# Weights loaded later, an opening in another order and an ending shared by two engines, in a recurrent-scan and gated-GLU kernel

## The chip, the cores and the metric

The kernel runs on one core of one Trainium2 chip. The metric is the device time of one execution in microseconds (us). A core has five engines that run side by side and wait for each other by semaphores: PE (matrix products), ACT (activations, copies with a scale), DVE (vector work), POOL (GpSimd, vector work out of on-chip memory) and SP (here it only issues DMAs). Each engine works through its own list of instructions strictly in order. PE's results land in eight PSUM banks, which ACT and DVE empty; POOL cannot read them.

## The reference

For x of 2048 tokens by 448 features (bfloat16), the kernel computes a diagonal complex recurrence and a gated two-layer network on the same normalised input, and joins them:

```
xn = layernorm(x)
Bu = xn @ B_bar.T                     # complex, 448 states; B_bar = (Lam_bar - 1) / Lam * B
h[t] = Lam_bar * h[t-1] + Bu[t]       # Lam_bar = exp(exp(log_dt) * Lambda)
s = 2 * Re(h @ C.T) + xn * Dskip
g = sigmoid(xn @ w_gate) * (xn @ w_up)        # 1792 wide
out = x + s * silu(g @ w_down)
```

## The kernel before, in words

**Tiling.** The 2048 tokens are four chunks `c` of 512 tokens; a chunk has four tiles `j` of 128 tokens. The 448 states are four blocks `pt` (three of 128, the last of 64 whose real and imaginary parts share the partitions). The 1792 hidden features are 14 blocks `ft` of 128.

**The recurrence without complex numbers.** Each state is turned by its own angle per token, so that the recurrence becomes a real one that DVE's scan does (`scan`, L597). The turning needs tables of cosines (`cosT`) and sines with both signs (`spm`) of 512 columns. They are built once: `emit_whole` or `frac_by` and `emit_frac` bring the angle into one turn, `emit_abs` takes its magnitude, `emit_sin` and `emit_cos` (ACT) give columns 256 to 511, `emit_neg` (L454, DVE) the negated sine, and `emit_mirror` (L457 to L460, POOL) copies the other half backwards.

**The products.** A pair of units runs on PE at a time (`duo`). A unit is either `gu_unit` (gate and up of one `ft`, 7 products each for upper and lower row halves) or `bu_unit` (Bu of one block `pt`). The upper 64 rows of one unit run beside the lower 64 of the other. Where a sum changes from one half to the other, the next product has to follow the other half's last one; the kernel brings this about with an instruction that does nothing on POOL (L520), which waits for PE and for which PE waits:

```
if self.half not in (None, half):
    word = pool.nop()
```

These words stand in POOL's list behind all that was written before them.

**Order of a chunk.** Chunk 0 opens with three, then four blocks by `gu_wholes` and `gu_halves` (L710, L703), then `emit_line(0, ...)`. Each later chunk runs gate/up units, Bu units, then `emit_downs` of the chunk before (the product with `w_down`, tile `wd`, sums `ds`) and `emit_ys` (the product with C, tile `ct`). DVE's work of the recurrence is cut into `pieces` that `fill` places between the units; `due` and `due_g` hold elementwise work that is written a little later. At the very end `keep_order` fixes the written order on every engine.

**Opening.** Tiles 0 and 1 of x are normalised with DVE's statistics (`ln_stats`), tiles 2 and 3 with ACT's sums (`ln_sum`, `ln_mean`, `ln_square`); POOL raises the variance to -1/2 (`ln_pow`, L238; `ln_pow_of` also adds the epsilon there, L246). `ln_norm` writes the normalised tile, `ln_turn` transposes it on PE into PSUM (`tps`, two banks) and `ln_out` (L280) copies it out. `rows` holds log_dt, Lambda_im and Lambda_re; PE transposes it into `tp_v`, and `emit_vecs` (L313) copies that. `warm` (L192) are products with the identity whose result nobody reads.

**Transfers.** Nearly all DMAs stand in SP's list, in written order. Among them, in the order before: x of chunk 0, weights in three parts (`load_w`), B, x of chunk 1, transposes of B (`emit_b`), the down weights (L1020), x of chunk 2, the transposes of chunk 1 (L270), C (`load_c`, planned at (0, 7)), the swap of the last block's halves (L538, L539), and the transposes of C (L169), which ACT (L490) scales and joins during the downs of chunk 0.

**End.** For the last chunk `empty` (L772) puts Silu on ACT; `emit_rest_of` (L847, L853) computes xn * Dskip * gate + x for tiles 0 to 2 on DVE; for each tile `emit_y` multiplies with C on PE and `emit_fin` (L865, L868, L869) multiplies the sum by the gate, adds the rest and sends the tile out. Tile 3 goes in two halves of 224 columns (3a, 3b below) and adds its skip part by a product with the identity on PE.

Of the kernel before, what the change touches and what calls it, by code (L numbers as in the profile page):

```python
# [10 lines left out]
FP32 = mybir.dt.float32  # L11
# [6 lines left out]
D = 448  # L18
F = 1792
P = 128  # L20
# [43 lines left out]
def kernel(  # L64
# [55 lines left out]
    def load_w(eng, f0, f1):  # L120
        for t, mat, p0 in ((wg, B_w_gate, 0), (wu, B_w_up, 64)):
            eng.dma_start(out=t[:, :, f0:f1], in_=mat[0:384, f0:f1].rearrange("(kt p) f -> p kt f", p=P))
            eng.dma_start(out=wt[p0:p0 + 64, f0:f1], in_=mat[384:448, f0:f1])

# [290 lines left out]
    def emit_whole(pt):  # L415
        whole = sp.tile([P, HC], I32, name="whole", tag=("ta", "tb")[pt % 2])
        act.activation(whole[:], iota_f[:], ACT.Copy, scale=K["turn"][:, pt:pt + 1])
        K[pt] = whole


    def frac_by(eng, pt, tag):
        t = sp.tile([P, HC], FP32, name="turns", tag=tag)
        eng.tensor_scalar(out=t[:], in0=iota_f[:], scalar1=K["turn"][:, pt:pt + 1], scalar2=None, op0=ALU.mult)
        f = sp.tile([P, HC], FP32, name="fracs", tag=tag)
        eng.tensor_scalar(out=f[:], in0=t[:], scalar1=MAGIC, scalar2=-MAGIC, op0=ALU.add, op1=ALU.add)
        eng.tensor_tensor(out=f[:], in0=t[:], in1=f[:], op=ALU.subtract)
        K[pt] = f

# [24 lines left out]
    def emit_neg(pt):  # L453
        dve.tensor_single_scalar(out=spm[:, pt, 1, HC:TC], in_=spm[:, pt, 0, HC:TC], scalar=-1.0, op=ALU.mult)  # L454

# [249 lines left out]

    def gu_wholes(c, ft, gt, ut, first, n0=0, n1=TC):
        f0, f1 = ft * P, (ft + 1) * P
        for t, wm in ((gt, wg), (ut, wu)):
# [53 lines left out]
    def emit_downs(c):  # L762
# [42 lines left out]

    def y_ops(c, j, rows, d0=0, d1=D, skipped=False):
        sl = slice(j * P, (j + 1) * P)
        o = [(ident[rows, :], xn[c % 3][rows, j, d0:d1], d0, d1)] if skipped else []
        for pt in range(3):
# [30 lines left out]

    rests = {}

    def emit_rest_of(c, j):
        if j == 3:
            return
        t = op_.tile([P, D], BF16, name="t_g", tag="zb", bufs=4)
        dve.tensor_tensor(out=t[:], in0=xn[c % 3][:, j, 0:D], in1=gs[c][:, j, :], op=ALU.mult)  # L847
        if not rests:
            for k, nm in ((0, "raw_re"), (2, "raw_im")):
                both = w.tile([P, 2, D], FP32, name="t_x", tag=nm)  # L850
                rests.update({k: both[:, 0, :], k + 1: both[:, 1, :]})
            del rests[3]
        dve.tensor_tensor(out=rests[j], in0=t[:], in1=x_t[c][:, j, :], op=ALU.add)  # L853

    def emit_y(c, j, d0=0, d1=D):
        ops = y_ops(c, j, slice(0, P), d0, d1, j not in rests)
        ys[c, j] = bank("y_ps", D)
# [4 lines left out]
    def emit_fin(c, j, d0=0, d1=D):  # L862
        tt = c * TPC + j
        sg = op_.tile([P, D], BF16, name="sg", tag="sigd", bufs=4)
        dve.tensor_tensor(out=sg[:, d0:d1], in0=ys[c, j][:, d0:d1], in1=gs[c][:, j, d0:d1], op=ALU.mult)  # L865
        o = op_.tile([P, D], BF16, name="o_l", tag="zb", bufs=4)
        also = rests[j] if j in rests else x_t[c][:, j, :]
        dve.tensor_tensor(out=o[:, d0:d1], in0=sg[:, d0:d1], in1=also[:, d0:d1], op=ALU.add)  # L868
        sync.dma_start(out=out_flat[tt * P:(tt + 1) * P, d0:d1], in_=o[:, d0:d1])  # L869
# [110 lines left out]
    for ft in range(4):  # L980
        gu_wholes(0, ft, *gus[ft], False, HC, TC)
    emit_frac(1)
    emit_abs(1)
    emit_steps()
    for pt in (0, 1, 3):
        emit_sin(pt)
        emit_cos(pt)
        emit_neg(pt)
        if pt == 0:
            emit_b_twice()  # L990
            emit_frac(3)
            emit_abs(3)
    emit_abs(2)
    ubs = [fp.tile([P, TC], BF16, name="ub") for _ in range(4)]
# [4 lines left out]
    for ft in range(4):  # L999
        gu_out(ft, gus[ft][0], ubs[ft])  # L1000
        up_copy(ft)
        if ft == 1:
# [128 lines left out]
```

## Time and profile before

| | us |
|---|---|
| median of 3 runs | 187.44 (187.14 to 188.24) |
| the profiled execution, whole | 186.7 |
| its span, first to last instruction | 184.6 |
| PE busy | 178.0 (96%) |
| DVE busy | 164.4 (89%) |
| ACT busy | 114.6 (62%) |
| POOL busy | 29.1 (16%) |

The span is what the timelines below count in, from 0; the 2.1 us between it and the profiled execution lie around it. The granted TensorE clock is 1.00 all through. The page says that PE's matmuls are pipelined and their ends modelled, so that a busy PE is not one at its peak; pauses are read from where a product starts. In a timeline a row gives the start, the time from first to last of the instructions merged in it, the engine, the line, the operation, output and inputs, shapes, their number, and in brackets how long the engine had been idle just before and what ended that. "PEld" is the load of a matmul's stationary operand; "POOLq" and "SPq" are what POOL's and SP's sequencers do themselves, such as the words of L520 and the issue of a DMA.

### The profile page before, as it was taken

The numbers are of one execution on the slowest core, as the hardware profiler recorded it, in microseconds if no ns is written. First come the engines' busy times: TensorE is split into PE (matmuls) and PEld (weight loads), VectorE is DVE, ScalarE is ACT, GpSimd is POOL, SyncE is SP. The second block draws the span as 40 slices with busy tenths as digits, with TensorE's granted clock in tenths as the row PEclk, the third lists the DMA queues.
The fourth block names the chain that finished last, engine by engine and source line by source line (L and its number), as shares of the span: only waits on it lengthen the run. The fifth ranks groups of instructions, "written<-read, shape, count | busy, mean of one in ns | idle before, by whom it ended". The sixth has DMA issues, their size and how long they took to land.

```text
span 184.6 us, 4475 instructions
## 1 busy us (share of the span) xinstructions
PE 178.0 (96%) x1706; PEld 101.4 (55%) x1706; DVE 164.4 (89%) x331; ACT 114.6 (62%) x238; POOL 29.1 (16%) x64
## 2 busy tenths in 40 slices
PE   6899999999999999999999999999999999999990
PEld 5676788545544444645554445545654445655560
DVE  3789979989999969999999999599999999699494
ACT  4889857899579686997367766067048657051300
POOL 3689368514000000004000000000000000000000
PEclk9999999999999999999999999999999999999999
DMA  5999999934332122011241010020000010020102
GB/s 152 301 317 219 253 351 190 236 78 99 82 78 57 28 45 87 4 51 51 48 71 28 4 28 0 4 99 0 5 14 14 4 24 10 0 80 23 28 25 75
DMA packets 27659, 15.07 MB, mean 82 GB/s; under 512 B 16243, under 2 KB 27638, under 8 KB 27638
## 3 DMA queue, kind: packets, MB, share of 16 engines
q1 hardware_dynamic: 27488, 14.67, 34.2%
q8 instruction: 13, 0.21, 0.5%
q10 hardware_dynamic: 150, 0.12, 0.2%
q14 instruction: 8, 0.07, 0.1%
HBM read 8.49 MB, written 1.84 MB: 56 GB/s over the span
## 4 chain that ended last, share of the span: by engine, by line
PE 83%; DVE 10%; DMA 3%; issue 1%; ACTq 1%; SPq 0%
PE g_ps L518 23%; PE u_ps L518 20%; PE d_ps L518 17%; PE bu L518 10%; PE y_ps L518 8%; DMA rows<-in_A_Lambda_re_dram 2%; PE g_ps L710 2%; PE u_ps L710 1%; DMA wsw<-wv 1%; DVE sg L865 1%; DVE o_t L835 1%; DVE t_x L853 1%; DVE o_l L868 1%; DVE hF L745 1%; DVE wv L658 1%
## 5 line engine op out<-in xcount | busy, mean ns | idle before, releaser
L518 PE MATMUL u_ps<-xnT,wu 64*128 64x512 bf16 x312 | 66.5, 376 | 0.0
L518 PE MATMUL g_ps<-xnT,wg 64*128 64x512 bf16 x312 | 59.4, 376 | 0.0
L748 ACT ACTIVATE sig<-g_ps 128x512 bf16<-128x512 f32 x52 | 29.3, 599 | 27.6 <-PE g_ps L518 27.6
L518 PE MATMUL bu<-xnT,bT 64*128 64x512 bf16 x196 | 45.3, 376 | 0.0
L518 PE MATMUL d_ps<-wd,hF 64*128 64x448 bf16 x448 | 43.9, 349 | 0.0
L518 PEld LDWEIGHTS <-hF 64*128 64x128 bf16 x448 | 24.9, 94 | 18.0 <-POOLq L520 0.7
L518 PEld LDWEIGHTS <-wu 64*128 64x128 bf16 x312 | 24.8, 94 | 17.1 <-POOLq L520 1.6
L518 PEld LDWEIGHTS <-wg 64*128 64x128 bf16 x312 | 22.0, 94 | 18.0 <-POOLq L520 2.7
L748 ACT CAST ub<-u_ps 128x512 bf16<-128x512 f32 x52 | 29.3, 609 | 0.0
L597 DVE TENSOR_TENSOR_SCAN wv<-r_col,st,ta 128x512 bf16<-128x512 f32 x18 | 22.6, 1275 | 0.1
L518 PE MATMUL y_ps<-ct,h 64*128 64x448 bf16 (+2 forms) x203 | 22.7, 343 | 0.0
L518 PEld LDWEIGHTS <-bT 64*128 64x128 bf16 x196 | 17.8, 94 | 7.7
L745 DVE TENSOR_TENSOR hF<-sig,ub 128x512 bf16<-128x512 bf16 x52 | 20.9, 416 | 1.2 <-ACT ub L748 1.0
L518 PE MATMUL g_ps<-xnT,wt 64*128 64x512 bf16 x52 | 19.6, 376 | 0.0
L518 PE MATMUL u_ps<-xnT,wt 64*128 64x512 bf16 x52 | 19.6, 376 | 0.0
L518 PEld LDWEIGHTS <-h 64*128 64x128 bf16 (+1 forms) x203 | 13.3, 95 | 8.2 <-issue 0.4
L578 ACT CAST bus<-bu 128x512 bf16<-128x512 f32 x24 | 14.5, 603 | 2.9 <-PE bu L518 2.9
L776 ACT ACTIVATE sigd<-d_ps 128x448 bf16<-128x448 f32 x12 | 6.6, 552 | 14.1 <-PE d_ps L518 14.1
L238 POOL TENSOR_TENSOR rsd<-ve,mhalf 128x4 f32<-128x4 f32 (+2 forms) x6 | 6.5, 1080 | 47.5 <-PE u_ps L518 40.4
L518 PEld LDWEIGHTS <-wt 64*128 64x128 bf16 x104 | 9.8, 94 | 5.0
L835 DVE TENSOR_TENSOR o_t<-y_ps,xn 128x448 bf16<-128x448 f32 x12 | 6.9, 618 | 3.5 <-PE y_ps L518 3.4
L591 DVE TENSOR_TENSOR ta<-ta,tb 128x1024 bf16<-128x1024 bf16 x12 | 8.3, 690 | 0.3
(162 smaller groups left out, 223.5 us busy)
## 6 DMA issues: line engine op xcount, KB each, us to landing
wd<-in_B_w_down_dram SPq DMA_DIRECT2D x1, 1568.0 KB
x<-in_A_x_dram SPq DMA_DIRECT2D x3, 448.0 KB, 6.9
out_dram<-o_t SPq DMA_DIRECT2D x6, 224.0 KB, 2.1
wg<-in_B_w_gate_dram SPq DMA_DIRECT2D x2, 384.0 KB, 4.5
wu<-in_B_w_up_dram SPq DMA_DIRECT2D x2, 384.0 KB, 4.9
wg<-in_B_w_gate_dram SPq DMA_DIRECT2D x1, 576.0 KB
wu<-in_B_w_up_dram SPq DMA_DIRECT2D x1, 576.0 KB, 7.0
bsw<-bus SPq DMA_DIRECT2D x8, 64.0 KB, 2.0
```

Of the source, the lines that this page charges most:

```text
L238: pool.tensor_tensor(out=rsd[:, t:t + n, :], in0=ve[:, t:t + n, :], in1=mhalf[:, 0:n, :], op=ALU.pow)
L518: m = pe.matmul(self.t[:, n0:n1], lhsT=lhsT, rhs=rhs, start=self.done == 1, stop=self.done == self.n)
L578: empty = [lambda cc=cc: act.copy(out=bus[:, cc, :], in_=pst[cc][:]) for cc in range(2)]
L591: dve.tensor_tensor(out=T["ta"][:], in0=T["ta"][:], in1=T["tb"][:], op=add)
L597: dve.tensor_tensor_scan(out=T["wv"][:, cc, :], data0=rb, data1=T["ta"][:, cc, :], initial=(0.0 if c == 0 else st[pt][:, cc, :]), op0=mul, ...
L658: dve.tensor_tensor_scan(out=T["wv"][:], data0=rb, data1=T["ta"][:], initial=(0.0 if c == 0 else st3[:]), op0=mul, op1=add)
L710: pe.matmul(t[:, n0:n1], lhsT=wm[:, kt, f0:f1], rhs=xnT[c][:, kt, n0:n1], start=(first and kt == 0), stop=(not first and kt == 2))
L745: dve.tensor_tensor(out=h[:], in0=sig[:], in1=ub[:], op=ALU.mult)
L748: u.empty = [lambda: act.activation(sig[:], gt[:], ACT.Sigmoid), lambda: act.copy(out=ub[:], in_=ut[:])]
L776: act.activation(sigd[:], ds[j][:], ACT.Sigmoid)
L835: dve.tensor_tensor(out=o[:, i, :], in0=ys[c, j + 2 * i][:], in1=xb[:, i, :], op=ALU.add)
L853: dve.tensor_tensor(out=rests[j], in0=t[:], in1=x_t[c][:, j, :], op=ALU.add)
```

## The change

The diff, with lines of mere plumbing left out:

```diff
     def load_w(eng, f0, f1):
-        for t, mat, p0 in ((wg, B_w_gate, 0), (wu, B_w_up, 64)):
+        for t, mat in ((wg, B_w_gate), (wu, B_w_up)):
             eng.dma_start(out=t[:, :, f0:f1], in_=mat[0:384, f0:f1].rearrange("(kt p) f -> p kt f", p=P))
+        for mat, p0 in ((B_w_gate, 0), (B_w_up, 64)):
             eng.dma_start(out=wt[p0:p0 + 64, f0:f1], in_=mat[384:448, f0:f1])
...
-    act.dma_start(out=x_t[0][:, 1, :], in_=x_src[:, 1, :])
+    sync.dma_start(out=x_t[0][:, 1, :], in_=x_src[:, 1, :])
...
-    def load_c():
+    def load_wd_c():
+        sync.dma_start(out=wd[:], in_=B_w_down.rearrange("(ft p) d -> p ft d", p=P))
...
-        whole = sp.tile([P, HC], I32, name="whole", tag=("ta", "tb")[pt % 2])
+        whole = sp.tile([P, HC], I32, name="whole", tag=("ta", "tb", "tcs", "tb")[pt])
...
-    def frac_by(eng, pt, tag):
...
     def emit_neg(pt):
-        dve.tensor_single_scalar(out=spm[:, pt, 1, HC:TC], in_=spm[:, pt, 0, HC:TC], scalar=-1.0, op=ALU.mult)
+        pool.tensor_single_scalar(out=spm[:, pt, 1, HC:TC], in_=spm[:, pt, 0, HC:TC], scalar=-1.0, op=ALU.mult)
...
+                if c == NCH - 1:
+                    if q == 2:
+                        pieces.pop(0)[1]()
+                    emit_gate()
+                    emit_gate()
...
     def emit_rest_of(c, j):
-        if j == 3:
-            return
+        eng = dve if j % 2 == 0 else pool
         t = op_.tile([P, D], BF16, name="t_g", tag="zb", bufs=4)
-        dve.tensor_tensor(out=t[:], in0=xn[c % 3][:, j, 0:D], in1=gs[c][:, j, :], op=ALU.mult)
+        eng.tensor_tensor(out=t[:], in0=xn[c % 3][:, j, 0:D], in1=gs[c][:, j, :], op=ALU.mult)
...
-        dve.tensor_tensor(out=rests[j], in0=t[:], in1=x_t[c][:, j, :], op=ALU.add)
+        eng.tensor_tensor(out=rests[j], in0=t[:], in1=x_t[c][:, j, :], op=ALU.add)
...
     def emit_fin(c, j, d0=0, d1=D):
-        dve.tensor_tensor(out=o[:, d0:d1], in0=sg[:, d0:d1], in1=also[:, d0:d1], op=ALU.add)
+        (pool if j == 1 else dve).tensor_tensor(out=o[:, d0:d1], in0=sg[:, d0:d1], in1=rests[j][:, d0:d1], op=ALU.add)
...
-    warm(26)
-    for t in range(2):
-        ln_stats(t)
-        ln_pow_of(t, 1, mv[:, t:t + 1, 1:2], 1.0)
+    warm(31)
+    ln_stats(0)
+    ln_pow_of(0, 1, mv[:, 0:1, 1:2], 1.0)
+    ln_stats(1)
+    ln_root(1, 1)
     ln_sum(2)
-    ln_sum(3)
     turn_twice(tp_v, rows, 3)
-    warm(6)
...
-    ln_mean(2, 2)
+    ln_mean(2, 1)
     ln_square(2)
-    ln_square(3)
-    warm(4)
+    ln_pow_of(2, 1, sums[:, 2:3, 1:2], 1.0 / D)
     ln_norm(0, 1)
     ln_turn(0, 1)
     warm(4)
     ln_out(0)
     ln_out(1)
+    ln_stats(3)
+    for pt in (0, 1, 3, 2):
+        emit_whole(pt)
     act.activation(K["r"][:], K["arg"][:], ACT.Exp)
-    for pt in (1, 3):
-        emit_whole(pt)
     act.activation(dummy[:], hpi[:], ACT.Silu)
-    ln_pow_of(2, 2, sums[:, 2:4, 1:2], 1.0 / D)
-    frac_by(dve, 0, "ta")
-    emit_abs(0)
-    frac_by(pool, 2, "tcs")
+    ln_pow_of(3, 1, mv[:, 3:4, 1:2], 1.0)
     gus = [(bank("g_ps"), bank("u_ps")) for _ in range(3)]
     for ft in range(3):
-        gu_wholes(0, ft, *gus[ft], True, 0, HC)
-    for j in (2, 3):
-        ln_norm(0, j)
-        ln_turn(0, j)
+        gu_wholes(0, ft, *gus[ft], True, 0, HC, (0,))
+    for ft in range(3):
+        gu_wholes(0, ft, *gus[ft], True, 0, HC, (1,))
+    ln_norm(0, 2)
+    ln_turn(0, 2)
+    emit_frac(0)
+    ln_norm(0, 3)
+    ln_turn(0, 3)
+    emit_abs(0)
+    emit_frac(1)
+    emit_abs(1)
     for j in (2, 3):
         ln_out(j)
+    emit_frac(3)
+    emit_abs(3)
+    emit_frac(2)
+    emit_abs(2)
...
-    emit_frac(1)
-    emit_abs(1)
     emit_steps()
     for pt in (0, 1, 3):
         emit_sin(pt)
         emit_cos(pt)
-        emit_neg(pt)
         if pt == 0:
             emit_b_twice()
-            emit_frac(3)
-            emit_abs(3)
-    emit_abs(2)
...
-    emit_neg(2)
     for pt in (0, 1, 3, 2):
+        emit_neg(pt)
         emit_mirror(pt)
...
-        if pt == 2:
-            sync.dma_start(out=wd[:], in_=B_w_down.rearrange("(ft p) d -> p ft d", p=P))
...
-    at(0, 7, 0.0, load_c)
+    at(0, 7, 0.0, load_wd_c)
```

What it does:

- **Opening, transfers.** Tile 1 of x moves from ACT's list to SP's second place, so that the three `rows` are first on ACT's. In each part of the weights the two large transfers stand ahead of the two small ones.
- **Opening, normalisation.** The variance of tile 1 is prepared on DVE (`ln_root`), tile 2 alone is summed by ACT, tile 3 gets DVE's statistics and a power of its own on POOL. All gate products of the first three blocks stand ahead of their up products.
- **Opening, tables.** All four blocks take `emit_whole` on ACT and `emit_frac` on DVE; the three-step `frac_by` of blocks 0 (DVE) and 2 (POOL) is gone. The four negations go from DVE to POOL, each ahead of its block's mirrors.
- **Down weights.** Their transfer goes from between the transposes of B to behind the transposes of chunk 1, just ahead of C.
- **End.** In the downs of the last chunk, rests 0 and 2 are written on DVE right behind their Silu, ahead of the last two steps of the recurrence; rests 1 and 3, with the one of tile 3 new, on POOL. The last addition of tile 1 is POOL's. Tile 3 no longer uses the identity product.

More of the change, by code (lines that the diff above doesn't have):

```diff
@@ L415, in emit_whole @@
     def emit_whole(pt):
-        whole = sp.tile([P, HC], I32, name="whole", tag=("ta", "tb")[pt % 2])
+        whole = sp.tile([P, HC], I32, name="whole", tag=("ta", "tb", "tcs", "tb")[pt])
         act.activation(whole[:], iota_f[:], ACT.Copy, scale=K["turn"][:, pt:pt + 1])
         K[pt] = whole
-    def frac_by(eng, pt, tag):
[L422 to L427, printed above, removed]
     def emit_frac(pt):
@@ L704, in gu_halves, with gu_wholes @@
                       rhs=xnT[c][p0:p0 + 64, 3, n0:n1], start=first, stop=not first)
-    def gu_wholes(c, ft, gt, ut, first, n0=0, n1=TC):
+    def gu_wholes(c, ft, gt, ut, first, n0=0, n1=TC, which=(0, 1)):
         f0, f1 = ft * P, (ft + 1) * P
-        for t, wm in ((gt, wg), (ut, wu)):
+        for t, wm in [((gt, wg), (ut, wu))[i] for i in which]:
             for kt in range(3):
@@ L804, with y_ops @@
     ys = {}
-    def y_ops(c, j, rows, d0=0, d1=D, skipped=False):
+    def y_ops(c, j, rows, d0=0, d1=D):
         sl = slice(j * P, (j + 1) * P)
-        o = [(ident[rows, :], xn[c % 3][rows, j, d0:d1], d0, d1)] if skipped else []
+        o = []
         for pt in range(3):
@@ L838, in emit_two @@
         sync.dma_start(out=out_t[:, c * TPC + j:(c + 1) * TPC:2, :], in_=o[:])
-    rests = {}
+    rests, room_of_rests = {}, {}
     def emit_rest_of(c, j):
-        if j == 3:
-            return
+        eng = dve if j % 2 == 0 else pool
         t = op_.tile([P, D], BF16, name="t_g", tag="zb", bufs=4)
-        dve.tensor_tensor(out=t[:], in0=xn[c % 3][:, j, 0:D], in1=gs[c][:, j, :], op=ALU.mult)
+        eng.tensor_tensor(out=t[:], in0=xn[c % 3][:, j, 0:D], in1=gs[c][:, j, :], op=ALU.mult)
         if not rests:
@@ L850, in emit_rest_of @@
                 both = w.tile([P, 2, D], FP32, name="t_x", tag=nm)
-                rests.update({k: both[:, 0, :], k + 1: both[:, 1, :]})
-            del rests[3]
-        dve.tensor_tensor(out=rests[j], in0=t[:], in1=x_t[c][:, j, :], op=ALU.add)
+                room_of_rests.update({k: both[:, 0, :], k + 1: both[:, 1, :]})
+        rests[j] = room_of_rests[j]
+        eng.tensor_tensor(out=rests[j], in0=t[:], in1=x_t[c][:, j, :], op=ALU.add)
     def emit_y(c, j, d0=0, d1=D):
-        ops = y_ops(c, j, slice(0, P), d0, d1, j not in rests)
+        ops = y_ops(c, j, slice(0, P), d0, d1)
         ys[c, j] = bank("y_ps", D)
@@ L865, in emit_fin @@
         dve.tensor_tensor(out=sg[:, d0:d1], in0=ys[c, j][:, d0:d1], in1=gs[c][:, j, d0:d1], op=ALU.mult)
-        o = op_.tile([P, D], BF16, name="o_l", tag="zb", bufs=4)
-        also = rests[j] if j in rests else x_t[c][:, j, :]
-        dve.tensor_tensor(out=o[:, d0:d1], in0=sg[:, d0:d1], in1=also[:, d0:d1], op=ALU.add)
+        if j == 3:
+            o = sp.tile([P, D], BF16, name="o_l", tag="ctmp")
+        else:
+            o = op_.tile([P, D], BF16, name="o_l", tag="zb", bufs=4)
+        (pool if j == 1 else dve).tensor_tensor(out=o[:, d0:d1], in0=sg[:, d0:d1], in1=rests[j][:, d0:d1], op=ALU.add)
         sync.dma_start(out=out_flat[tt * P:(tt + 1) * P, d0:d1], in_=o[:, d0:d1])
```

## The prediction

> **What bounds the kernel now.** First the engines' shares and the chain that ended last (parts 1 and 4 of the page), then the waits by total time.
>
> ```profile
> PE 178.0 (96%) x1706; PEld 101.4 (55%) x1706; DVE 164.4 (89%) x331; ACT 114.6 (62%) x238; POOL 29.1 (16%) x64
> PE 83%; DVE 10%; DMA 3%; issue 1%; ACTq 1%; SPq 0%
> PEld L518 <- POOLq L520: 5.0, 15, 0.5
> ```
>
> PE bounds it: from 7.69 us (first product) to 180.46 its matmuls follow each other without a pause of over 0.4 us. So an opening shorter by some time is a kernel shorter by that, a PE pause anywhere is paid in full, and the end behind PE's last sums counts on its own. The third line is the one to keep in mind: L520 is the Pool `nop` that stands between the two row halves of a sum, so a matmul waits until Pool's queue has come to it. POOL is 16% busy over the span, but not where these words stand first. The timelines of the weight loads, DVE and POOL show it:
>
> ```profile
> 16.37 0.33 DVE L454 TENSOR_SCALAR spm<-spm 128x256 bf16<-128x256 bf16 x1
> 16.81 0.42 PEld L518 LDWEIGHTS <-wg 64*128 64x128 bf16 x6 [0.40 <-POOLq L520]
> 19.34 0.66 POOL L353 TENSOR_SCALAR smT<-sn 128x4 f32<-128x4 f32 x1
> 20.10 0.42 PEld L518 LDWEIGHTS <-wg 64*128 64x128 bf16 x6 [0.49 <-POOLq L520]
> ```
>
> The last table's negation ends on DVE at 16.70; the mirror L459 behind it in Pool's queue waits for that, the first `nop` stands behind the mirrors, and the weights load at 16.81. The next `nop` stands behind smT (ends 20.00), and PE goes on at 20.10. Twice PE lost some 0.2 us here to Pool's queue, although three mirrors were only queued, not yet done, when the first `nop` passed.
>
> Prices of Pool's work, from POOL's and DVE's timelines:
>
> ```profile
> 8.83 0.99 POOL L423 TENSOR_SCALAR turns<-iota_f,turn 128x256 f32<-128x256 f32 x1
> 9.90 1.10 POOL L425 TENSOR_SCALAR fracs<-turns 128x256 f32<-128x256 f32 x1
> 11.08 0.73 POOL L426 TENSOR_TENSOR fracs<-turns,fracs 128x256 f32<-128x256 f32 x1
> 11.09 1.00 DVE L431 SCALAR_TENSOR_TENSOR frac<-iota_f,turn,whole 128x256 f32<-128x256 f32 x1
> 12.47 0.48 DVE L431 SCALAR_TENSOR_TENSOR frac<-iota_f,turn,whole 128x256 f32<-128x256 f32 x1
> 16.56 0.40 POOL L460 COPY spm<-spm 128x255 bf16<-128x255 bf16 x1
> 16.61 3.29 DVE L720 SCALAR_TENSOR_TENSOR hF<-tanh,ub 128x512 bf16<-128x512 f32 x4
> 16.90 0.86 POOL L457 COPY cosT<-cosT 128x255 bf16<-128x255 bf16 x1
> ```
>
> A Pool copy of 255 columns takes 0.40 alone and 0.86 beside DVE's hF; DVE's L431 takes 1.00 beside a Pool tensor-tensor, 0.48 without.
>
> **Opening, before the products.** The second tile's variance goes from Pool to DVE, so its power runs straight behind the first tile's (4.46 to 5.04) and ends at about 5.65 instead of 5.96. The rows lose one issue ahead of them (0.41 us) and no longer push `vec` into that gap. Tile 1 moves to SP's second place: issued at 1.17, landing 2.7 later at 3.9, before DVE asks at 4.0. The second normalisation moves from 5.99 to 5.68, the first product from 7.69 to about 7.35: -0.35. Five warming matmuls more and ten fewer lie in waits. Gate first, up weights second give the up weights 1 us more; their issue also comes 0.8 earlier, as one transfer less is ahead.
>
> Third and fourth tile: their statistics no longer share ScalarE; I find the second `ln_out` pair ending at 11.05 (11.17 before), after frac 0, abs 0, frac 1 and abs 1 on DVE (1.54 together), just in front of the fourth tile's up products. The -0.35 survives to there. Two more `whole` on ACT (0.45 each) replace one square and one sum (0.67, 0.58): even.
>
> **Opening, Pool.** It loses three operations (0.99+1.10+0.73) and gains four negations of 128x256, one ahead of each table's mirrors, all ahead of the first `nop`. The spm mirror now waits for Pool's own negation, so the queue no longer runs ahead: the `nop` passes when the last negation is done. Pool can start at about 11.0 (fourth tile's power ending near 9.1, then the five small operations that took 11.75 to 13.81 before). Three tables and a negation are 3 x (N + 0.08 + 3 x 0.35) + N. PE wants the `nop` at 16.63 - 0.35 = 16.3. N is not in the trace. The nearest row is the same operation, L423, at 0.99; the lower bound is the copy, 0.40. The Trainium skill, GPSIMD Engine Reference, section Engine selection, says that one-input work on this engine is roughly line-rate; by that N would be the copy's 0.40, while L423 and L425, with one input each, disagree. With N = 0.85 (nearer to L423, which stood partly beside DVE's work) the negation ends at 11.0 + 5.94 + 0.85 = 17.8; from 15.8 on the hF of four tiles lie beside it (four at 0.82), which stretch the last three copies by up to 0.46 each: 19.2. I take 18.6: PE waits 2.3. Bounds: N = 0.40 ends at 16.0, no wait, not even the 0.2 of before; N = 0.99 with all of the stretching gives 20.0, a wait of 3.7. DVE is relieved of four negations (0.22 each) and four of the fractions' steps, none of which PE waited for.
>
> **Down weights.** They go from SP's 21.44 to behind chunk 1's turns (before: 26.52 to 32.73), so are issued at about 32. 1.57 MB at the 360 GB/s of 24 to 28 us is 4.4 us: landed near 38.5, wanted by the first d_ps at 42.2. Cover 3.5 us: nothing. Queued behind them: C's loads (0.9 MB, 3 us of transfer, then complete near 41.5, not 38), the swap of chunk 0's last table (DVE reads it at 57.5), and the eight turns of C, which began at 39.51 and would begin 0.4 to 1.2 later. ACT waits for these:
>
> ```profile
> 53.59 0.67 ACT L490 ACTIVATE c_tmp<-tc_im,nci 128x448 f32<-128x448 bf16 x1 [1.20 <-DMA tc_im<-c_im]
> ```
>
> Behind that wait it empties two d_ps banks (until 56.54), which the pair (4, -3) takes at about 56.8: 0.3 us of room. If PE is late by 2 us from the opening, all of this is covered: 0. If it is not, 0 to 1.2.
>
> **End.** DVE loses rest 1 (0.38 + 0.62) and the o_l of tile 1; the skip matmuls (2 x 0.1) go. Rests 0 and 2 (about 1.9 from ACT's Silu at 172.7) go into the wait for wsw (until 173.5) and push td and h by some 1.15, to 175.56; y's seventh matmul wants h at 175.92: 0.36 of room. Pool gets rest 1, rest 3 and the o_l of tile 1: five tensor-tensors of 448. No Pool tensor-tensor of that size is in the trace; from L426 with the 0.19 of tiny ones as fixed part, 0.19 + 448 x (0.73 - 0.19)/256 = 1.14. The lines that they must fit between:
>
> ```profile
> 174.89 0.98 ACT L772 ACTIVATE g_t<-d_ps 128x448 bf16<-128x448 f32 x2 [1.67 <-PE d_ps L518]
> 178.52 3.94 SPq L869 DMA_DIRECT2D out_dram<-o_l  x5
> 181.83 0.28 DVE L868 TENSOR_TENSOR o_l<-sg,x 128x224 bf16<-128x224 bf16 x1
> ```
>
> From Silu of tile 1 (175.45) five at 1.14 with 0.3 of gaps end at 181.45. Then SP issues tile 1, 3a and 3b, in that order and 0.4 apart, and the last lands 1.5 later: 183.85, where the last o_l of before (182.11) landed at 183.6. That is +0.2 by the time of PE. Contention adds: DVE's o_l of tiles 0 and 2 have two inputs in SBUF, as L431 has, and L431 lost 0.52 beside L426. The Trainium skill, SBUF — State Buffer, section Who interferes with whom, has the two engines hold one port pair exclusively, each for its whole instruction; by that rule L431 would have lost 0.73, and both sides lose in turn. By the row Pool's chain grows by about 1.05 (two times 0.52): +1.25. If a Pool tensor-tensor cost only a copy's rate (0.19 + 448 x 0.82 ns = 0.56), Pool would not decide: DVE's last o_l ends at 180.95, -1.2. I take +0.9, nearer to the rows of this kind.
>
> **Sum.** -0.35 + 2.3 + 0 + 0.9 = +2.85 on the profiled execution of 186.7 (span 184.6 and 2.1 around it). That run lies 0.7 under the median of the runs shown, 187.44, and the same difference on the median gives 190.3.
>
> **Rivals.**
> 1. Pool's negation costs a copy (N = 0.40). For it: L457 to L460 move as many columns of the same type in 0.40. Against: L423 and L425, and that neither copies nor scales. It is also what the page named above would give. Then the opening keeps -0.35, the room of 0.3 at 56 us takes 0 to 1.2 of it back, and the end costs 0.2 to 1.25: 187.3 to 189, at about 188.2.
> 2. The other side: Pool is cheap at both places. Its negations run at the copy's rate and its tensor-tensors under about 0.9 each, so that the o_l of tile 1 is done before 3b's (the point is 181.3 by the time of PE, where SP's three issues close as late as before). Then -0.35, another -0.25 since smT no longer holds the second `nop`, and -1.2 at the end: 185.6. For it: Pool is idle for 84% of the span, DVE sits idle 2.5 us for wsw and then works without a gap to the end. Against: the 0.73 of L426 for 256 columns.
> 3. Pool's `nop` comes in time, but the turns of C come late (C's loads behind the weights): -0.35 + 1.2 + 0.9 gives 189.2 without any wait on Pool. For it: ACT already waits 1.2 there. Against: that landing is itself late by more than its 2.4 us median, so some of the 1.2 may be chance.
> 4. Pool's wait as priced, the end cheap: 2.3 - 0.35 - 1.2 = +0.75, 188.2.
>
> **How the numbers follow.** The forecast (Pool holds the first `nop` for 1 to 3.7 us, and the end costs something) has 0.62, from the measured 0.99, 1.10, 0.73 and the 0.86 beside hF. Rival 1 has 0.15, half of it within 0.5%, half above; rival 2 has 0.10; rival 3 0.05; rival 4 0.08, all within 0.5%. A measurement of this kernel tells about 0.5% (0.94 us) from no change. Faster 0.10 (rival 2); same 0.16 (half of rival 1 and rival 4); slower 0.74. The range goes up to 192.4: a wait of 3.7 and an end of +1.25 give 187.4 + 4.6 = 192.0, and a little for what an idle PE may lose after it. Down it goes to 186.9, which leaves out rival 2 alone. The forecast's own range is 188.8 to 192.0.
>
> **What would show it.** Right: on POOL the four negations at 0.8 to 1 us each, the last ending after 17 us; PE idle behind POOLq for over 1 us in the first pair of the opening; first product near 7.35; behind the last d_ps, five Pool tensor-tensors of over 1 us, with DVE's o_l stretched beside them, and SP's tile 1 issue after 181.5 by the old count. Wrong: negations at 0.4 and the first pair without a pause; tile 1's o_l finished before 3b's; a PE pause near 42 us on the down weights, or near 56 us on a bank.

## The result

The changed kernel takes 189.93 us (median of 19 runs, 187.33 to 190.25), the kernel before 187.29 us on the same chips (median of 19, 185.93 to 188.36): a ratio of 1.0105, 95% interval [1.0071, 1.0138], so slower by 1.05%. The prediction was 190.3, slower. Here and below a median is of all runs, while a ratio and its interval leave out runs more than 1.5% above the fastest of their kernel.

The runs of the changed kernel fall into two groups: 13 of 19 lie between 189.71 and 190.25 with a granted clock of 0.985 to 0.988, five between 187.33 and 188.31 with 0.994 to 0.997, and one (188.62, 0.986) between them. Its first trace (profiled execution 188.31, span 186.5) is of the rarer group. One more run of the same kernel, e10 below, gave a trace of the commoner one (189.96, span 188.2); where the two differ, e10 is the one that explains the median.

First e10's page, the shares, the clock's slices and the chain that ended last, and a line of its waits:

```profile
PE 179.5 (95%) x1699; PEld 102.5 (54%) x1699; DVE 164.3 (87%) x326; ACT 113.8 (60%) x236; POOL 33.1 (18%) x71
PEclk9999699999999999999999999999999999999998
PE 85%; POOL 7%; issue 5%; DVE 2%; POOLq 0%
PEld L511 <- POOLq L513: 6.8, 13, 2.9
```

POOL, absent from the chain of before, now carries 7% of it. The fifth slice of the clock, 18.8 to 23.5 us, stands at 6. The words of L513 (L520 before) cost the weight loads 6.8 us in all, one of them 2.9; before it was 5.0, and at most 0.5. The place, in PE's timeline of e10 (start, duration, engine, line, operation, count; in brackets the idle time before it):

```profile
6.87 1.14 PE L703 MATMUL g_ps<-xnT,wg 128*128 128x256 bf16 x9 [0.19 <-DVE xnT L282]
14.54 0.82 PE L511 MATMUL g_ps<-xnT,wg 64*128 64x512 bf16 x6
18.65 1.17 PE L511 MATMUL g_ps<-xnT,wg 64*128 64x512 bf16 x6 [2.42 <-POOLq L513]
19.62 1.72 PE L511 MATMUL u_ps<-xnT,wu 64*128 64x512 bf16 x6
21.14 1.62 PE L511 MATMUL g_ps<-xnT,wg 64*128 64x512 bf16 x6
22.60 0.93 PE L511 MATMUL u_ps<-xnT,wu 64*128 64x512 bf16 x6
```

POOL's timeline of e10, the negations (L447) and the mirror ahead of the last of them:

```profile
10.38 0.87 POOL L447 TENSOR_SCALAR spm<-spm 128x256 bf16<-128x256 bf16 x1
14.49 0.84 POOL L447 TENSOR_SCALAR spm<-spm 128x256 bf16<-128x256 bf16 x1
16.43 0.86 POOL L453 COPY spm<-spm 128x255 bf16<-128x255 bf16 x1
17.26 1.28 POOL L447 TENSOR_SCALAR spm<-spm 128x256 bf16<-128x256 bf16 x1
```

PE comes to the loop at 14.54, 0.68 earlier than before (15.22). The second half of its first pair would start at 16.05; Pool's last negation ends at 18.54, and the products start at 18.65. Then comes a second payment: 64x512 products that go six in 0.81 to 1.02 at full rate take 1.17 to 1.72. The two stretches 18.65 to 21.14 and 21.14 to 23.37 last 2.49 and 2.23 us, where such a stretch takes 1.51: 0.98 + 0.72 = 1.70 us more. So the opening's account in e10 is -0.68 + 2.51 (the hold beyond the gap that before had there) + 1.70, less some 0.2 that the second word, behind smT, cost before: +3.3, and the next pair, with the first Bu products, starts at 24.88 instead of 21.62. The rest of the 3.6 us between the two spans is the end's.

The first trace shows the other group; the same rows of PE's timeline:

```profile
7.26 2.08 PE L703 MATMUL g_ps<-xnT,wg 128*128 128x256 bf16 x9
9.13 1.75 PE L703 MATMUL u_ps<-xnT,wu 128*128 128x256 bf16 x9
16.29 0.82 PE L511 MATMUL g_ps<-xnT,wg 64*128 64x512 bf16 x6
```

Here the first 18 products run at about half rate (7.26 to 10.72, 3.46 us; 1.96 before), PE reaches the loop only at 16.29 and asks for the word at 17.8, after the last negation (17.58). The slow opening hides Pool: nothing is held, no second slow stretch follows, and the run is 1.6 us *shorter* than the common one.

The end, from POOL's timeline of e10:

```profile
178.75 1.03 POOL L847 TENSOR_TENSOR t_g<-xn,g_t 128x448 bf16<-128x448 bf16 x1 [89.54 <-ACT g_t L765]
179.85 1.03 POOL L853 TENSOR_TENSOR t_x<-t_g,x 128x448 f32<-128x448 bf16 x1
180.84 1.42 POOL L847 TENSOR_TENSOR t_g<-xn,g_t 128x448 bf16<-128x448 bf16 x1
183.59 1.03 POOL L870 TENSOR_TENSOR o_l<-sg,t_x 128x448 bf16<-128x448 bf16 x1
```

DVE's o_l in the same trace:

```profile
180.21 1.15 DVE L870 TENSOR_TENSOR o_l<-sg,t_x 128x448 bf16<-128x448 bf16 x1
181.93 0.81 DVE L870 TENSOR_TENSOR o_l<-sg,t_x 128x448 bf16<-128x448 bf16 x1
183.67 1.20 DVE L870 TENSOR_TENSOR o_l<-sg,t_x 128x224 bf16<-128x224 bf16 x1
185.20 0.39 DVE L870 TENSOR_TENSOR o_l<-sg,t_x 128x224 bf16<-128x224 bf16 x1
```

Pool's operations of 448 columns take 1.03 where least disturbed, up to 1.42 beside DVE, and DVE's o_l of 448 columns, 0.62 before, takes 1.15 and 0.81 beside them; the one of 224 columns takes 1.20 beside Pool's o_l and 0.39 behind it. From the first product with C to the end of the last o_l it was 7.33 us before (174.78 to 182.11) and is 7.58 here (178.01 to 185.59): +0.25.

### The profile page after: what moved, and what is told of

It is laid out like the page before. It is cut to its first block, busy times and chain, and to the rows that moved or that the text cites. A ratio compares the mean times of both kernels' runs of the same rounds, so it can differ in the third digit from the quotient of the medians.

```text
span 186.5 us, 4470 instructions
## 1 busy us (share of the span) xinstructions
PE 180.0 (97%) x1699; PEld 96.1 (52%) x1699; DVE 164.2 (88%) x326; ACT 114.0 (61%) x236; POOL 34.2 (18%) x71
## 3 DMA queue, kind: packets, MB, share of 16 engines
q1 hardware_dynamic: 27632, 14.79, 32.7%
## 4 chain that ended last, share of the span: by engine, by line
PE 71%; SPq 8%; DMA 6%; issue 6%; POOL 2%; DVE 2%; ACT 1%; POOLq 0%; ACTq 0%
PE g_ps L511 18%; PE u_ps L511 16%; PE d_ps L511 14%; PE y_ps L511 8%; PE bu L511 6%; SPq L171 5%; DMA c_re<-in_A_C_im_dram 5%; SPq L272 2%; PE warm_ps L194 2%; PE g_ps L703 2%; DMA tc_im<-c_im 2%; PE u_ps L703 2%; DVE o_l L870 1%; POOL t_g L847 1%; POOL t_x L853 1%
## 5 line engine op out<-in xcount | busy, mean ns | idle before, releaser
L511 PE MATMUL u_ps<-xnT,wu 64*128 64x512 bf16 x312 | 66.9, 376 | 0.5 <-ACT zb L771 0.5
L511 PE MATMUL g_ps<-xnT,wg 64*128 64x512 bf16 x312 | 59.0, 376 | 0.0
L511 PE MATMUL bu<-xnT,bT 64*128 64x512 bf16 x196 | 45.5, 376 | 0.0
L511 PE MATMUL d_ps<-wd,hF 64*128 64x448 bf16 x448 | 43.9, 349 | 0.0
L511 PEld LDWEIGHTS <-hF 64*128 64x128 bf16 x448 | 25.0, 94 | 18.0 <-POOLq L513 0.7
L511 PEld LDWEIGHTS <-wu 64*128 64x128 bf16 x312 | 24.0, 94 | 19.2 <-POOLq L513 1.6
L511 PEld LDWEIGHTS <-wg 64*128 64x128 bf16 x312 | 21.1, 94 | 18.3 <-POOLq L513 1.8
L511 PEld LDWEIGHTS <-bT 64*128 64x128 bf16 x196 | 17.8, 94 | 11.5 <-issue 0.8
L590 DVE TENSOR_TENSOR_SCAN wv<-r_col,st,ta 128x512 bf16<-128x512 f32 x18 | 22.6, 1275 | 0.1
L511 PE MATMUL y_ps<-ct,h 64*128 64x448 bf16 (+2 forms) x203 | 22.5, 343 | 0.0
L511 PE MATMUL g_ps<-xnT,wt 64*128 64x512 bf16 x52 | 19.6, 376 | 0.0
L511 PE MATMUL u_ps<-xnT,wt 64*128 64x512 bf16 x52 | 19.6, 376 | 0.0
L847 POOL TENSOR_TENSOR t_g<-xn,g_t 128x448 bf16<-128x448 bf16 x2 | 2.5, 1225 | 89.5 <-ACT g_t L765 89.5
L511 PEld LDWEIGHTS <-h 64*128 64x128 bf16 (+1 forms) x203 | 13.3, 95 | 8.3 <-issue 0.4
L240 POOL TENSOR_TENSOR rsd<-ve,mhalf 128x1 f32<-128x1 f32 (+1 forms) x7 | 6.3, 903 | 49.7 <-PE u_ps L511 46.5
L511 PEld LDWEIGHTS <-wt 64*128 64x128 bf16 x104 | 9.8, 94 | 5.6
```

Of the source, the lines that this page charges most:

```text
L240: pool.tensor_tensor(out=rsd[:, t:t + n, :], in0=ve[:, t:t + n, :], in1=mhalf[:, 0:n, :], op=ALU.pow)
L511: m = pe.matmul(self.t[:, n0:n1], lhsT=lhsT, rhs=rhs, start=self.done == 1, stop=self.done == self.n)
L590: dve.tensor_tensor_scan(out=T["wv"][:, cc, :], data0=rb, data1=T["ta"][:, cc, :], initial=(0.0 if c == 0 else st[pt][:, cc, :]), op0=mul, ...
L847: eng.tensor_tensor(out=t[:], in0=xn[c % 3][:, j, 0:D], in1=gs[c][:, j, :], op=ALU.mult)
```

## The experiments

Below, "the changed kernel" is the one of the prediction; its lines have other numbers where an edit shifts them. The letters in the expectations stand for theories. A is read from the first trace, and differs by run: the loss is the clock in the opening (e1, and in e3 that this hides Pool's word), the late turns of C (e2), a cheaper end (e4). E, from e5 on, is the prediction's as e2's and e3's traces bore it out: Pool's word holds PE, with what follows from it in each run. F and H say what makes a word late; the other letters are rivals within their own run. The runs were made on several chips, so each ratio is to the kernel before on the same chip, and small differences of medians between runs say little.

**e1: the warming products as before.**

```
-    warm(31)
+    warm(26)
     turn_twice(tp_v, rows, 3)
+    warm(6)
...
+    warm(4)
     ln_norm(0, 1)
```

> The changed kernel with its warming products as they stood before (26, 6, 4 and 4 in place of 31 and 4). Theory A (the loss is mostly TensorE's clock, which stays at half speed through the first 18 products because the products between the turns are gone): the 18 products of 256 columns take 1.96 us again instead of 3.46, the granted clock is 0.995 or more in nearly all runs, PE reaches the first pair of the loop near 14.9 us, and then Pool's word, which passes at 17.6 when the last negation ends, holds PE for about 1.2 us; the median falls from 189.9 to about 188.0. Rival B (the prediction's: Pool's word is the loss and the clock a chance): 18 products and clocks spread as in the changed kernel, median 189.5 to 190. Rival C (the rate of the clock hangs on when the run starts, not on the warming): same as B in the time, with the same two groups of times.

Measured: 189.06 us (6 runs, 188.31 to 190.79), ratio to before 1.0110 [1.0058, 1.0162]. The clock went from 0.985 to 0.997 and the times stayed in two groups. In its trace (span 186.5) the 18 products are slow all the same (7.79 to 11.2), and with five warming products more in all the first one comes 0.5 later than in the first trace. Theory A falls: the number of these products is not the cause. What decides in which runs the opening is slow stays open; the kernel before seems to have it too, with runs at a clock of 0.994 to 0.997 that lie mostly at 187.2 to 188.6, and runs at 1.0 mostly at 186.0 to 187.3.

**e2: the down weights early.**

```
     def load_wd_c():
-        sync.dma_start(out=wd[:], in_=B_w_down.rearrange("(ft p) d -> p ft d", p=P))
...
             load_w(sync, 1024, F)
+        if pt == 2:
+            sync.dma_start(out=wd[:], in_=B_w_down.rearrange("(ft p) d -> p ft d", p=P))
```

> The changed kernel with the down weights issued where they were before (ahead of chunk 0's loop). Theory A (C's loads and turns stand behind the down weights and come 2.4 us late, so that ScalarE waits 2.5 us for tc_im and empties the banks late): the turns of tc_re begin near 39.5 again, ScalarE's wait for tc_im falls to about 1.2, the PE pauses of 0.33 and 0.87 at 57 to 58.5 us go, median about 0.9 lower than the changed kernel. The prediction's working (the move is covered): no difference, within 0.2.

Measured: 189.91 (12 runs, 187.67 to 190.16), ratio 1.0094 [1.0056, 1.0133], against 189.93 for the changed kernel: nothing, as the prediction's working said, and e2's theory A falls. Its trace was the first of the common group: loop at 14.53, held 2.42, half clock behind it.

**e3: negations on VectorE**, called where they were before.

```
-        pool.tensor_single_scalar(out=spm[:, pt, 1, HC:TC], in_=spm[:, pt, 0, HC:TC], scalar=-1.0, op=ALU.mult)
+        dve.tensor_single_scalar(out=spm[:, pt, 1, HC:TC], in_=spm[:, pt, 0, HC:TC], scalar=-1.0, op=ALU.mult)
...
         emit_cos(pt)
+        emit_neg(pt)
```

> The changed kernel with the four negations on VectorE again. Prediction's working (Pool's negations hold PE for 2.3 us): 2.3 lower. Theory A (PE is late by more than that from its clock, so Pool's word is never waited for): within 0.3 of the changed kernel, PE still at the first pair near 16.3 and not held there for more than 0.2.

Measured: 187.05 (12 runs, 185.54 to 188.28), ratio 0.9987 [0.9952, 1.0021]: 2.9 us less than the changed kernel. Theory A was wrong, the prediction's part right, and undersized by the slow stretch behind the hold. PE reaches the loop at 14.53 and is not held: the halves of its first two pairs start 1.51 or 1.52 apart.

**e4: the old end.** `emit_rest_of`, `emit_fin`, `y_ops` and the end of `emit_downs` as in the kernel before; of it:

```
-        eng = dve if j % 2 == 0 else pool
+        if j == 3:
+            return
...
-        (pool if j == 1 else dve).tensor_tensor(out=o[:, d0:d1], in0=sg[:, d0:d1], in1=rests[j][:, d0:d1], op=ALU.add)
+        dve.tensor_tensor(out=o[:, d0:d1], in0=sg[:, d0:d1], in1=also[:, d0:d1], op=ALU.add)
```

> The changed kernel with the end of the kernel before (rests by VectorE alone, skip of the last tile on TensorE, all o_l on VectorE). Prediction's working: 0.9 lower. Theory A, from the trace of after (last o_l only 0.27 later in PE's frame): 0.3 lower. Rival D (Pool cheap, VectorE relieved): 0.5 or more higher.

Measured: 187.47 (12 runs, 186.80 to 190.02), ratio 1.0020 [0.9982, 1.0059]. The median can't be read as the price of the end: eight of its twelve runs show a clock of 0.995 to 0.999, the group in which Pool's word isn't paid for, five of nineteen in the changed kernel. Its four others take 189.07 to 190.02, against 189.71 to 190.25. So the three expectations stay undecided by the times. The traces give the price in a frame of their own: first product with C to last o_l is 7.37 here and 7.33 before; over all traces it is 6.92 to 7.37 with the old end (five) and 7.58 to 7.60 with the new one (nine).

**e5: Pool's negations ahead of all mirrors.** The same work on Pool in another order.

```
     for pt in (0, 1, 3, 2):
         emit_neg(pt)
+    for pt in (0, 1, 3, 2):
         emit_mirror(pt)
```

> The changed kernel with Pool's four negations one after the other, ahead of all mirrors; the same work on Pool. Theory E (in most runs PE is on time at 16.05 and Pool's word holds it 2.4 us, because each mirror waits for Pool's own negation and the last negation ends at 18.5; the wait is a matter of Pool's order, not of its work): the last negation ends near 14.9 (four at 0.87 from 10.4, the fourth sine ready at 13.97), the word passes there, no pause of PE in the first pair, median about 187.1, as with the negations on VectorE. Rival F (the word passes only when all but about three of the operations ahead of it are done): 12 mirrors still stand ahead of it, it passes near 18.5 and the median stays at 189.9.

Measured: 191.10 (6 runs, 189.44 to 191.42), ratio 1.0168 [1.0130, 1.0206]: worse, and neither theory was right. Its trace has the slow opening (loop at 16.16), so PE wants the first word only behind the last negation (16.53). Rows of POOL's timeline of e5, the third mirror and sT:

```profile
17.15 0.86 POOL L453 COPY spm<-spm 128x255 bf16<-128x255 bf16 x1
22.76 0.18 POOL L358 TENSOR_TENSOR sT<-smT,sgn 128x1 f32<-128x1 f32 x1
```

PE's timeline of e5, the first products behind either word:

```profile
17.68 0.81 PE L511 MATMUL g_ps<-xnT,wg 64*128 64x512 bf16 x6
22.77 0.91 PE L511 MATMUL g_ps<-xnT,wg 64*128 64x512 bf16 x6 [1.91 <-POOLq L513]
```

At 17.68 Pool is in its third mirror of twelve, and the first word has passed: the nine behind it needn't be done, so F is wrong. But the second word, wanted at 20.7, passes at 22.77, when sT starts. sT reads smT, which Pool itself has just written, behind all mirrors. That suggested theory H: a word is held by the last instruction ahead of it that must still wait for something, be it Pool's own result. The second payment comes here too: from 23.7 to 27.1 the granted clock is 0.50.

**e9: negations and constants ahead of the mirrors.** As e5, and:

```
         emit_neg(pt)
+    emit_constants()
     for pt in (0, 1, 3, 2):
...
-    for ft, cost, fn in ((5, 0.0, emit_constants), (8, 0.0, emit_den), (9, 0.1, emit_inv), (9, 0.0, emit_a),
+    for ft, cost, fn in ((8, 0.0, emit_den), (9, 0.1, emit_inv), (9, 0.0, emit_a),
```

> As the run with the four negations first, and the small operations on smT and sT, which also wait for Pool's own results, moved ahead of the mirrors as well. Theory H (a word passes as soon as no operation ahead of it in Pool's queue still has to wait, however many mirrors are queued; so the two words of the opening are held by the last negation and by sT, not by the mirrors' work): the first word passes near 15 us, the second is not held, although Pool copies mirrors until about 22 us; no PE pause, granted clock 0.994 or more, median 187.1, as with the negations on VectorE. Rival F (the mirrors ahead of the word must be done): 191 again, PE held 2 us or more in the second pair.

Measured: 186.65 (10 runs, 186.27 to 189.57), ratio 0.9966 [0.9922, 1.0010]: 3.3 us less than the changed kernel with the same work on Pool; from the kernel before it can't be told apart. POOL's timeline of e9, the last negation, sT and the last mirror:

```profile
14.31 0.85 POOL L447 TENSOR_SCALAR spm<-spm 128x256 bf16<-128x256 bf16 x1 [0.94 <-ACT spm L435]
15.44 0.19 POOL L358 TENSOR_TENSOR sT<-smT,sgn 128x1 f32<-128x1 f32 x1
21.19 0.40 POOL L453 COPY spm<-spm 128x255 bf16<-128x255 bf16 x1
```

PE's timeline of e9, the products behind the two words:

```profile
16.31 0.81 PE L511 MATMUL g_ps<-xnT,wg 64*128 64x512 bf16 x6
19.33 0.81 PE L511 MATMUL g_ps<-xnT,wg 64*128 64x512 bf16 x6
```

Both words are through while Pool goes on copying until 21.6; the two halves that were held start on time, 1.52 and 1.51 behind their first halves (14.79 and 17.82). F falls and H holds: at 16.31 Pool is in the first of its twelve mirrors. The dear thing was the order on Pool, not the 3.6 us of negations (2.74 for three, 0.85).

**e11: the negations alone, in the kernel before.** They leave the loop of `emit_sin` and `emit_cos`, and:

```
-        dve.tensor_single_scalar(out=spm[:, pt, 1, HC:TC], in_=spm[:, pt, 0, HC:TC], scalar=-1.0, op=ALU.mult)
+        pool.tensor_single_scalar(out=spm[:, pt, 1, HC:TC], in_=spm[:, pt, 0, HC:TC], scalar=-1.0, op=ALU.mult)
...
     for pt in (0, 1, 3, 2):
+        emit_neg(pt)
         emit_mirror(pt)
```

> The kernel before, with its four negations given to Pool, each just ahead of its mirrors, and nothing else of the change. The prediction's way of working: Pool's small operations end at 13.8 there, three tables and a negation end at about 22, where PE wants the word at 16.7: held some 5 us, and 1.7 more at half clock behind it: about 194 (192.5 to 194.5). Rival (Pool's negations were dear only beside the rest of the change): 187.4 to 188.5.

Measured: 191.13 (5 runs, 189.92 to 192.96), ratio 1.0143 [1.0040, 1.0246]: 3.3 us lost by this one edit on the medians, 2.7 by the ratio, less than expected but far from the rival. The five runs lie at 189.92 to 191.13 (clock 0.994 or 0.995) and at 192.91 and 192.96 (0.991 and 0.985), which is inside the expected range. Its trace is of the lower group. There the opening happened to be late (loop at 16.61), the last negation ends at 21.49, the word is held 3.30 and the products behind it run at full rate, so the 1.7 isn't paid there.

**e8: the hold filled with work.** 40 products of a tile of zeros are added to the waiting sum ahead of the held product.

```
+            if spare and self.half not in (None, half):
+                spare.pop()
+                for _ in range(40):
+                    pe.matmul(self.t[:, 0:P], lhsT=ident[:], rhs=zero[:], start=False, stop=False)
             m = pe.matmul(self.t[:, n0:n1], lhsT=lhsT, rhs=rhs, start=self.done == 1, stop=self.done == self.n)
```

`spare` has one entry, so this happens once, at the first change of halves.

> The changed kernel with 40 products of zeros of 128 columns (about 0.056 us each at full clock, 2.2 us in all) put on TensorE just ahead of the first product that waits for Pool's word; they add zero to the sum. Theory E (the pause is paid twice: 2.4 us of waiting, then 1.7 us of products at half clock, because TensorE stood idle): where PE is on time, the two pairs behind the wait take 1.5 us each instead of 2.85 and 1.9, and those runs come down from 189.9 to about 188.2, with a granted clock of 0.995 or more in place of 0.985. Rival G (the clock falls for another reason, as its windows happen to stand): clock and time as in the changed kernel.

Measured: 188.63 (11 runs, 188.20 to 189.99), ratio 1.0084 [1.0055, 1.0114], and the clock at 0.997 to 1.0 in every run; 188.2 was expected. PE's timeline of e8, the held product and the next stretch (L519 is the L511 of the others):

```profile
18.61 0.92 PE L519 MATMUL g_ps<-xnT,wg 64*128 64x512 bf16 x6
20.14 0.90 PE L519 MATMUL g_ps<-xnT,wg 64*128 64x512 bf16 x6
```

It still waits until 18.6, but the stretch behind takes 1.53 instead of 2.49. So the slow stretch comes from TensorE standing idle, rival G falls, and the stretch is a price of its own: 0.96 us in the first stretch behind the hold, 1.3 us on the medians. The two ratios' intervals overlap, and three of e8's runs took 189.63 to 189.99 at a clock of 0.999; no trace shows why. The Trainium skill, TensorE: Matmul & The Clock Gate, section What's actually happening, says that the array runs at half clock until it has been busy through one window of some 3.4 us, and that these windows run free of the kernel's start. This case agrees in the size of the slow stretch: the granted clock is 0.50 for some 3.4 us in e10 (19.2 to 22.6), e2 (18.8 to 22.2) and e5 (23.7 to 27.1). It begins 0.2 to 1.0 us behind the first product after the hold, and an idle time of 2.42 us, in e5 of 1.91, shorter than such a window, was enough to bring it about; 3.30 us in e11 were not. So the length of a hold alone doesn't decide. Free-running windows would fit that, as a hold may fall across two of them, and they are a candidate for the two kinds of opening too, but no run here settles either.

**e10: the changed kernel again.** No edit.

> The changed kernel itself once more, for a trace of its commoner group of times (13 of 19 runs near 190 with a granted clock of 0.985 to 0.988; its first trace is of the other group, 188.3 at 0.994). Theory: 189.9, first pair at 14.5, PE held about 2.4 us by Pool's word, then two pairs at half clock; no pause near 57 us. If the trace falls in the rarer group again: first pair near 16.3 and no hold.

Measured: 189.93 (8 runs, 187.48 to 190.28), ratio 1.0082 [1.0025, 1.0139]; its trace is the one read above, and has no pause near 57 us.

**e6 and e7: what is left when parts are undone.** e6 is e3 with the early down weights; e7 is e6 with the old end, so only the opening's other edits remain.

> Negations on VectorE and the down weights at their old place; the opening's other edits and the new end stay. With PE no longer held in the opening, the late turns of C cost a pause of 0.87 us near 55.7 us (seen with the negations on VectorE alone, 0.6 more than the ordinary gap of 0.27). Theory E: that pause goes, median 0.6 under the 187.05 of the negations alone: 186.45. Rival (the turns' lateness is covered): 187.0.

> Only the opening of the change is left: negations on VectorE, down weights at the old place, the old end. Theory E: first product near 6.85 and first pair at 14.53, 0.69 earlier than in the kernel before, nothing given back in the middle, the end 0.25 shorter than with the new one: 186.2 against 187.4 before (ratio 0.994). Rival (the gap in the middle is that of before, where ScalarE's wait for C's turns already had no room): the 0.69 is given back near 55 us, 187.3.

Measured: e6 186.93 (12 runs, 186.13 to 187.51), ratio 0.9978 [0.9954, 1.0001]; e7 186.57 (10 runs, 185.20 to 187.38), ratio 0.9940 [0.9905, 0.9975]. The pause near 56 us of e3 (two products 0.86 apart instead of 0.21) is in neither trace. On the medians e6 gains 0.1 over e3, less than the runs can tell and nearer to its rival than to E, and e6's trace has a pause of its own (0.57 at 22.55, on the up weights of the third part). In e7's trace the first product starts at 7.18 and the loop at 14.85, 0.3 later than expected, and its median lies above the 186.2 of E and below the 187.3 of the rival. e7 is faster than the kernel before: the opening's edits are worth 0.8 us on the medians when nothing takes them back.

**e12: the best of it.** e9 with the early down weights and the old end.

> The opening of the change with Pool's negations first and the constants ahead of the mirrors, the down weights at their old place and the old end: every part that cost something mended or undone, and Pool keeps the negations. The kernel with only the opening left and the negations on VectorE had a ratio of 0.994 [0.9905, 0.9975]. Theory H: the same here, 186.2 to 186.6, no hold by Pool's word, no pause near 56 us, last output as in the kernel before. Rival (Pool's mirrors, which now end near 21.5, are late for the first table's readers): 187.3 or more.

Measured: 185.93 (12 runs, 184.87 to 187.38), ratio 0.9957 [0.9922, 0.9993] to a before of 187.22. Its trace has no hold by a word and no pause near 56 us, as H said. Faster than both kernels; from e7 it can't be told apart.

## Why the prediction was right, and where its working was off

**Opening, before the products: -0.35 forecast.** Right in sign, small in size. First product 6.87 in e10 (7.69 before) and loop at 14.54 (15.22): -0.68 at the loop. In the other traces of the new opening at full rate the loop starts at 14.40 to 14.90, so the gain is 0.3 to 0.8. In the traces with the slow opening the first product starts at 7.26 to 7.79, and nothing is gained at the loop. What the forecast missed is the first tile of x. It took over that tile's landing unchanged, but DVE's statistics of it begin earlier:

```profile
3.25 0.63 DVE L208 BATCH_NORM_STATS2 stats<-x 128x6 f32<-128x448 bf16 x1 [1.75 <-DMA x<-in_A_x_dram]
2.81 0.63 DVE L210 BATCH_NORM_STATS2 stats<-x 128x6 f32<-128x448 bf16 x1 [1.32 <-DMA x<-in_A_x_dram]
```

The first row is of the kernel before, the second of e10. All twelve traces of the new opening have 2.63 to 2.86 there, the two of the old one 3.25. That points to tile 1, which no longer goes out from ACT's list at the same moment; no run undoes this edit alone, so it is not shown.

**Pool holds the first word: 2.3 forecast.** Confirmed in the common group by its own numbers: negations at 0.84 to 0.87 alone (0.85 was taken), the last one at 1.28 beside DVE's hF, its end at 18.54 (18.6 forecast), the hold 2.42 us by the row. e3 removes it and 2.9 us go. That it didn't show in the first trace was chance of that run. The agreement to 0.1 us is in part luck: Pool begins the negations at 10.38, not at 11.0, and the work beside it stretches its queue by 1.4 us, not by 0.8. The upper bound is misadded: 18.35 with N = 0.99 and three copies stretched by 0.46 make 19.7, not 20.0. The reason given, that the queue stops at what must wait for Pool's own negation, fits e5 and e9, where words pass with nine and eleven mirrors undone once those waits are over. The sum left out the second word, which stands behind smT and sT under the same rule: the 0.2 that it cost before is not paid in e10, where PE comes late.

**The clock behind the hold: not in the sum.** The working allowed "a little for what an idle PE may lose" in the range alone. It measured 1.70 us in e10, and e8 ties it to the idle time. This is the term that was missing, and the largest error of the working.

**Down weights: 0 forecast.** Right for the kernel as it stands, and for the reason given: e2 changes nothing, because PE is late by then. The turns of C do begin late: at 40.02 in e3 and 41.95 in the first trace, whose PE is itself 1.1 us late, against 39.51 before; 0.4 to 1.2 later was forecast. ACT shows it in the first trace, and PE, which waits for a bank that ACT empties:

```profile
55.46 0.67 ACT L483 ACTIVATE c_tmp<-tc_im,nci 128x448 f32<-128x448 bf16 x1 [2.47 <-DMA tc_im<-c_im]
58.45 0.37 PE L511 MATMUL u_ps<-xnT,wu 64*128 64x512 bf16 x1 [0.49 <-ACT zb L771]
```

In four traces with the weights late and PE not held (the first one, e1, e3, e9) two products there stand 0.74 to 0.87 apart, 0.5 to 0.7 over the usual 0.21; in a fifth (e4) they don't. With the weights early (e2, e6, e7, e12) none do, and with PE held for 2.4 us (e10, e8) neither. That is rival 3's mechanism at half its price, hidden in the common runs by the wait for Pool's word, which rival 3 takes as absent.

**End: +0.9 forecast, +0.25 measured** (7.58 against 7.33). The mechanism was there and its size was not. Pool's tensor-tensors cost 1.03 where 1.14 was taken, and DVE beside them adds 0.65 in all where 1.05 was taken. So tile 1's o_l ends at 184.62, which in PE's time of before (3.23 us earlier) is 181.4: the forecast's chain without contention, where 182.5 with it was expected. DVE's last o_l ends at 185.59 and decides. DVE had been relieved by rest 1 and one o_l and used that room for its stretched ones.

**Sum.** Forecast -0.35 + 2.3 + 0 + 0.9 = 2.85. By e10's rows: -0.68 + 2.51 + 1.70 - 0.2 (smT's word of before) + 0.25 = 3.6, which is what lies between the spans of e10 (188.2) and before (184.6). The median moved by less, 2.64: the whole executions of these two traces lie 3.26 apart (the time around the span is 1.8 us in e10, 2.1 before), and the trace of before (186.7) is itself one of its shorter runs, 0.6 under its median. The forecast of 190.3 came near 189.93 with one term missing (1.7) and two that were taken too high: the end by 0.65, the opening by 0.33. That these errors nearly cancel is luck; that Pool's word is the largest term is not.

## What to carry to other kernels

On POOL here, an instruction that only passes a word through the queue was late by the last wait ahead of it, not by the work ahead of it. So write what must wait, for the engine's own results too, ahead of the long copies, and let the copies follow: the words then pass while the copies are still to be done. A hold of TensorE is paid twice where the clock falls behind it, so price it with the slow stretch. Before a trace is believed, compare its execution's time and clock with the median: the first trace here was of the rarer kind and pointed to the wrong cause.

## What had not been expected of the hardware

- A word passed Pool's queue with nine copies of 0.40 to 0.86 us still undone ahead of it (e5), and with eleven in e9; only an unfinished wait held it.
- Idle TensorE for 2.4 us cost 1.7 us more at half clock (e10), and 40 products of zeros in the gap prevented it (granted clock 0.985 to 0.988 against 0.997 to 1.0). An idle 1.91 us in e5 was followed by it too; a longer hold in e11, 3.30 us, wasn't, and no run tells why.
- The same opening ran its first 18 products in 1.96 us in some traces and in 3.3 to 3.6 us in others (2.3 in e11), whatever the number of warming products.
- DVE's addition of 224 columns took 1.20 us beside a Pool tensor-tensor, 0.39 beside none. In e10 each of DVE's three stretched additions lost the rest of the Pool instruction that it began in, less 0.14: 0.53 of 0.67, 0.19 of 0.33, 0.81 of 0.95. That fits the exclusive hold of the shared port that the prediction drew on from the Trainium skill, SBUF — State Buffer, section Who interferes with whom, better than a fixed 0.52 for each meeting, which the forecast took from one row.
